# One branch behind the attention instead of three, the attention's bias on ScalarE, and the root's first operation moved

## The chip, the cores and the metric

The kernel runs on one core of a Trainium2 chip. The metric is the device time of one execution in microseconds (us). A core has five engines with queues of their own: TensorE (PE in the profile; its weight loads are PEld), VectorE (DVE), ScalarE (ACT), GpSimd (POOL) and SyncE (SP, which issues most transfers). An instruction runs when it is at the head of its engine's queue and the semaphores that it waits for have been raised by other engines or by transfers.

## The reference, cut to what matters

```python
def _attn_ref(q, k, v, n_global, n_local):          # batch 2, 8 heads, 768 positions, head_dim 64
    scores = scale * np.matmul(q, k.transpose(0, 1, 3, 2))
    is_global = pos[None, :] < int(n_global)        # 8
    is_local = (rel >= 0) & (rel < int(n_local))    # 96; rel = query position - key position
    dist = np.where(is_global & ~is_local, float(n_local), np.abs(rel))
    scores = scores - slopes[:, None, None] * dist
    scores = np.where(is_global | is_local, scores, -1000000000.0)
    a = softmax(scores)
    return np.matmul(a, v)

def _moe_ref(x, w_gate, w_val, w_out, rms_g):       # 1536 tokens, 512 -> 1536 -> 512
    xn = x / np.sqrt(np.mean(x * x, -1) + 1e-06) * rms_g
    g = xn @ w_gate
    return (silu(g) * (xn @ w_val)) @ w_out

def _moe2_ref(x, w_skip, w_gate, w1, w2):           # 8 experts, 512 -> 1024 -> 512, one per kept token
    ...
```

The two numbers n_global and n_local are inputs. The kernel has a windowed path for n_local up to 97 and n_global up to 32, and a general path for all other values. With the inputs that are timed (8 and 96) the general path is skipped.

## The kernel before, in words

The program is one long straight line in which the author fixes the order on each engine by the order of the Python calls. It has four stages, which the profile separates by time: the windowed attention (to about 99 us), the first products of the gated layer with the RMS statistics (to about 125 us), the rest of the gated layer and of the routing, and the experts.

**The start.** `load_ints` (L39) fetches the two integers, `consts` (L44 to L79) turns them into floats `gl` on DVE, and five small DVE operations (L70 to L76) make `fasti`, 1 when the windowed path applies. `values_load` (L77) reads it into a register of every engine, and `tc.If(flag == 0)` (L985) skips `general_attention`. `bias_tiles` (L94 to L117), a generator, then makes on DVE, from the table `rel` (576 columns of distances, 576 of key numbers, 8 slopes; L978 loads it), a mask `keep` and `miss`, a clipped distance, and for each of four pairs of heads four pieces of `bias` (L112), one `next` for a pair.

**The attention.** `attention` (L192 to L390) is a generator too. It works on 24 items (8 pairs of heads, 3 groups of 256 queries). In step t it issues the scores of item t on PE (`qk`, L240), transposes of item t-2 (`trans`, L286), the product with the values of item t-3 (`pv`, L313); on DVE the normalization of item t-1 (L267, L271, L278) and for item t four score operations (`ttr`, L251: score plus bias, and the row's extreme `m`); on ACT the exponentials (`exp`, L262). `tick()` between DVE operations takes one step of another generator, `s.small`: there the root of the RMS statistics is put among the score operations.

**The statistics.** `Rms.stats(g)` sums squares by PE products with ones (L444). Called with 3 it issues the first DVE operation of the root, `rv` (L448), at once. `Rms.root` (L450) is the generator of what follows: 11 small DVE operations on 128 x 6 and six diagonal tiles `rd`, three on DVE (L469) and three on ACT (L472). `spread` (L474) multiplies these with ones on PE (L478), and ACT copies the result to `rs` (L481).

**Behind the attention.** In the last steps PE begins the products of the gated layer (`gemm1`, L538); `gate1` (L549 to L556) closes each on DVE and ACT, one product behind (`behind`). A second `tc.If` stood after step 16 (L1048), a third after the attention (L1065); both use the register loaded at the start. Behind the third come the root of the second half, the fourth product, and `spread`.

Of the kernel before, what the change touches and what calls it, by code (L numbers as in the profile page):

```python
# [18 lines left out]
NEG = -1.0e9  # L19
# [24 lines left out]
def consts(s, ints):  # L44
# [23 lines left out]
    s.ng, s.nl = s.gl[:, 0:1], s.gl[:, 1:2]  # L68
    a = c.tile([128, 3], F32, name="fasta")
# [24 lines left out]
def bias_tiles(s):  # L94

    nc = s.nc
    s.kinds = [0, 64, 192, 384]
# [3 lines left out]
    keep, miss, slopes = s.keep, s.miss, s.slopes  # L103
    nc.gpsimd.tensor_copy(slopes, s.rel[:, 2 * N:])
    spans = [(0, 64, 0), (64, 192, 4), (192, 384, 0), (384, 576, 4)]
# [12 lines left out]
def general_attention(s):  # L118

    nc, tc = s.nc, s.tc  # L120
    with tc.tile_pool(name="ga", bufs=1) as p, tc.tile_pool(name="gap", bufs=1, space=PSUM) as ps:
        slopes = p.tile([128, 8, 2], F32, name="gslopes")
        for j in range(16):
            nc.gpsimd.memset(slopes[:, j // 2, j % 2:j % 2 + 1], -(2.0 ** -(j % 8 + 1)))
        with tc.For_i(0, 8, 1) as pr:
            slope = p.tile([128, 2], F32, name="gslope")
            nc.vector.tensor_copy(slope, slopes[:, ds(pr, 1), :].rearrange("p a b -> p (a b)"))
            for hh in range(2):
                r = slice(64 * hh, 64 * hh + 64)
                q = p.tile([64, 768], F32, name="gq")  # L130
                nc.sync.dma_start(q.rearrange("p (a n) -> p a n", a=1),
                                  s.qx.rearrange("a p n -> p a n")[r, ds(pr, 1), :])
                k = p.tile([64, 928], F32, name="gk")
                nc.sync.dma_start(k.rearrange("p (a n) -> p a n", a=1),
                                  s.kx.rearrange("a p n -> p a n")[r, ds(pr, 1), :])
                v = p.tile([128, 11, 64], F32, name="gv")
                nc.sync.dma_start(v.rearrange("p (a b) d -> p a b d", a=1),
                                  s.vx.rearrange("a p h b d -> p a h b d")[:, ds(pr, 1), hh])
                xo = p.tile([64, 768], F32, name="gxo")
                rel0 = p.tile([128, 768], F32, name="grel0")  # L140
                nc.gpsimd.iota(rel0, pattern=[[-1, 768]], base=0, channel_multiplier=1,
                               allow_small_or_imprecise_dtypes=True)
                key0 = p.tile([128, 768], F32, name="gkey0")
                nc.gpsimd.iota(key0, pattern=[[1, 768]], base=0, channel_multiplier=0,
                               allow_small_or_imprecise_dtypes=True)
                with tc.For_i(0, 6, 1) as i:
                    qi = p.tile([64, 128], F32, name="gqi")
                    nc.vector.tensor_scalar(qi.rearrange("p (a c) -> p a c", a=1),
                                            q.rearrange("p (i c) -> p i c", c=128)[:, ds(i, 1), :],
                                            0.125, None, ALU.mult)  # L150
                    rel = p.tile([128, 768], F32, name="grel")
                    nc.vector.tensor_copy(rel, rel0)
                    key = p.tile([128, 768], F32, name="gkey")
                    nc.vector.tensor_copy(key, key0)
                    loc = p.tile([128, 768], F32, name="gloc")
                    dist, keep = distance(s, rel, key, loc)
                    sc = ps.tile([128, 6, 128], F32, name="gsc")
                    for j in range(6):
                        nc.tensor.matmul(sc[:, j, :], lhsT=qi, rhs=k[:, 160 * j:160 * j + 128],
                                         start=True, stop=True)  # L160
                    t = p.tile([128, 768], F32, name="gt")
                    nc.vector.scalar_tensor_tensor(
                        out=t, in0=dist, scalar=slope[:, hh:hh + 1], in1=sc.rearrange("p a b -> p (a b)"),
                        op0=ALU.mult, op1=ALU.add)
                    nc.vector.tensor_tensor(t, t, keep, ALU.mult)
                    nc.vector.tensor_scalar(keep, keep, 1.0, -NEG, ALU.subtract, ALU.mult)
                    nc.vector.tensor_tensor(t, t, keep, ALU.add)
                    m = p.tile([128, 1], F32, name="gm")
                    nc.vector.tensor_reduce(m, t, AX.X, ALU.max)
                    nc.vector.tensor_scalar(t, t, m, None, ALU.subtract)  # L170
                    z = p.tile([128, 1], F32, name="gz")
                    nc.scalar.activation(t, t, AF.Exp, accum_out=z)
                    nc.vector.tensor_scalar(z, z, 1e-9, None, ALU.add)
                    nc.vector.reciprocal(z, z)
                    nc.vector.tensor_scalar(t, t, z, None, ALU.mult)
                    pt = ps.tile([128, 6, 128], F32, name="gpt")
                    for j in range(6):
                        nc.tensor.transpose(pt[:, j, :], t[:, 128 * j:128 * j + 128], s.ident)
                    pts = loc.rearrange("p (a b) -> p a b", a=6)
                    nc.vector.tensor_copy(pts, pt)  # L180
                    po = ps.tile([64, 128], F32, name="gpo")
                    for j in range(6):
                        nc.tensor.matmul(po, lhsT=v[:, 2 * j, :], rhs=pts[:, j, :],
                                         start=j == 0, stop=j == 5)
                    nc.vector.tensor_copy(xo.rearrange("p (i c) -> p i c", c=128)[:, ds(i, 1), :],
                                          po.rearrange("p (a c) -> p a c", a=1))
                    nc.vector.tensor_scalar(rel0, rel0, 128.0, None, ALU.add)
                nc.sync.dma_start(s.xg.rearrange("(a h p) n -> p a h n", h=2, p=64)[:, ds(pr, 1), hh, :],
                                  xo.rearrange("p (a n) -> p a n", a=1))
# [203 lines left out]
class Rms:  # L393
# [30 lines left out]
    def general(self, xg):  # L424

        s, nc = self.s, self.s.nc
        for hp in range(4):
# [3 lines left out]
            sq = self.sq[hp] if hp < 2 else s.rpool.tile([128, 768], F32, name="gsq", bufs=1)  # L431
# [3 lines left out]
            if hp > 1:  # L435
                nc.vector.tensor_tensor(self.sq[1], self.sq[1], sq, ALU.add)

    def stats(self, g, psum=None):
# [7 lines left out]
        if g == 3:  # L446
            self.v = s.rpool.tile([128, 6], F32, name="rv", bufs=2)
            nc.vector.tensor_scalar(self.v, self.ss[:, 0:6], 1.0 / 512.0, 1e-6, ALU.mult, ALU.add)  # L448

    def root(self):  # L450

        s, nc, v = self.s, self.s.nc, self.v
        r = s.r[self.b] = s.cpool.tile([128, 6], F32, name=f"r{self.b}")
# [12 lines left out]
        d = self.diag = s.rpool.tile([128, 6, 128], F32, name="rd", tag="sq", bufs=4)  # L466
# [475 lines left out]
def attn_moe_kernel(ctx, tc, qx, kx, vx, rel, ints, wgv, w_out, rms_g, w9, w9t, w1, w2, out):  # L942
# [33 lines left out]
    s.keep = s.apool.tile([128, 576], F16, name="keep", bufs=1)  # L976
# [4 lines left out]
    s.miss = s.apool.tile([128, 576], F32, name="miss", bufs=1)  # L981
# [44 lines left out]
    def step1(x, *parts, silu=True):  # L1026

        gemm1(s, *x)
        run(*parts, *[gate1(s, *behind.pop(0), silu) for _ in behind[:1]])
        behind.append(x)  # L1030

    def gemm1s():
        z = done[0]
        done[0] += 1
# [396 lines left out]
```

## Time and profile before

| | us |
|---|---|
| median of 3 runs (lowest, highest) | 554.08 (553.87, 554.45) |
| the profiled execution, its own time | 554.08 |
| its span, from first to last instruction | 552.3 |
| PE busy in the span | 524.2 (95%) |
| DVE busy | 404.8 (73%) |
| ACT busy | 277.5 (50%) |
| POOL busy | 140.8 (25%) |

The span is 1.8 us shorter than the execution's own time, and that execution's time is the median of the runs. Busy time is an average over the four stages; what a stage is bound by is read from its own stretch. In rows of the timeline the columns are the start in the span, the length, engine, line, operation, tiles, sizes and count, and in brackets the idle time of that engine just before with what ended it.

### The profile page before, as it was taken

To read this page: it belongs to the slowest core of one execution; us is meant where nothing else is said; L and a number is where in the kernel's file an instruction comes from. 1 tells how busy PE (TensorE), PEld (TensorE's weight loads), DVE (VectorE), ACT (ScalarE), POOL (GpSimd) and SP (SyncE) were. 2 spreads that over 40 slices of the span, in tenths; PEclk is the share of its full clock that TensorE was granted. 3 is DMA by queue.
4 is the path that set the end of the run, shared out by engine and by line. 5 is a ranking of instruction groups with operands and counts; after the bars stand their busy time and mean duration, and the time that the engine had idled before them with its cause. 6 is when DMAs were issued, how large, how long until landed. Compare 5 with 4: busy or idle time off the path is not lost. (4 is left out here: it accounts for less than half of the span.)

```text
span 552.3 us, 9096 instructions
## 1 busy us (share of the span) xinstructions
PE 524.2 (95%) x3132; PEld 425.8 (77%) x3132; DVE 404.8 (73%) x1026; ACT 277.5 (50%) x631; POOL 140.8 (25%) x140
## 2 busy tenths in 40 slices
PE   3899886999999999999999999999999999999994
PEld 2676665878888888888888888878789787888883
DVE  5899999567888688868884358456443599999971
ACT  2799896324332233333333255244231587988850
POOL 2446545001222212212220200000000512666001
PEclk9999998999999999999999999999999999999998
DMA  8653511112323323323313512116171599999300
GB/s 301 210 211 139 173 36 39 33 46 77 105 88 113 113 79 114 114 79 113 115 38 130 214 39 78 39 52 215 39 293 57 202 393 395 398 399 396 131 15 16
DMA packets 28997, 80.62 MB, mean 146 GB/s; under 512 B 3512, under 2 KB 3768, under 8 KB 28945
## 3 DMA queue, kind: packets, MB, share of 16 engines
q1 hardware_dynamic: 24400, 68.61, 35.0%
q0 software_dynamic: 2672, 8.22, 3.9%
q10 hardware_dynamic: 1872, 3.15, 1.6%
q8 instruction: 26, 0.43, 0.3%
q14 instruction: 27, 0.21, 0.1%
HBM read 72.28 MB, written 8.65 MB: 147 GB/s over the span
## 5 line engine op out<-in xcount | busy, mean ns | idle before, releaser
L538 PE MATMUL ps<-xh,wh 128*128 128x512 f32 (+1 forms) x304 | 115.4, 380 | 0.1
L538 PE MATMUL ps<-xh,wl 128*128 128x512 f32 (+1 forms) x304 | 115.0, 378 | 0.5 <-POOL wl L504 0.5
L538 PE MATMUL ps<-xl,wh 128*128 128x512 f32 (+1 forms) x304 | 114.9, 378 | 0.0
L854 DVE TENSOR_TENSOR ewl<-eraw,ewh 128x1024 fp32r<-128x1024 f32 x72 | 83.5, 1220 | 6.2 <-ACT ewh L845 5.9
L845 ACT CAST ewh<-eraw 128x1024 fp32r<-128x1024 f32 x72 | 71.3, 1055 | 6.2 <-DVE ewl L854 4.2
L538 PEld LDWEIGHTS ps<-xh,wl 128*128 128x128 f32 x304 | 57.2, 188 | 11.6 <-POOL wl L504 0.9
L491 DVE SCALAR_TENSOR_TENSOR wraw<-f64t,wraw 128x512 f32<-128x512 f32 x36 | 44.7, 1241 | 28.8 <-ACT f64t L489 28.8
L538 PEld LDWEIGHTS ps<-xh,wh 128*128 128x128 f32 x304 | 57.2, 188 | 11.0 <-issue 0.7
L538 PEld LDWEIGHTS ps<-xl,wh 128*128 128x128 f32 x304 | 57.2, 188 | 10.6
L604 PE MATMUL px<-woh,hh 128*128 128x512 f32 (+1 forms) x156 | 61.8, 396 | 0.0
L604 PE MATMUL px<-woh,hl 128*128 128x512 f32 (+1 forms) x156 | 58.7, 376 | 0.0
L604 PE MATMUL px<-wol,hh 128*128 128x512 f32 (+1 forms) x156 | 58.2, 373 | 0.0
L504 POOL TENSOR_TENSOR wl<-f64t,wh 128x512 fp32r<-128x512 f32 x24 | 31.0, 1293 | 101.3 <-ACT wh L503 55.7
L503 ACT CAST wh<-f64t 128x512 fp32r<-128x512 f32 x24 | 14.9, 622 | 71.4 <-DVE f64t L501 68.1
L262 ACT ACTIVATE es<-es,m 128x192 f32<-128x192 f32 (+1 forms) x96 | 41.4, 434 | 11.5 <-DVE m L251 10.3
L278 POOL TENSOR_SCALAR es<-es,z 128x192 f32<-128x192 f32 x46 | 36.0, 791 | 36.2 <-ACT pts L297 11.7
L286 PE MATMUL pt<-ident,es 128*128 128x128 f32 x176 | 30.5, 305 | 10.1 <-DVE pts L295 6.6
L286 PEld LDWEIGHTS pt<-ident,es 128*128 128x128 f32 x176 | 20.7, 152 | 21.6 <-DVE pts L295 10.0
L568 DVE TENSOR_TENSOR hl<-h,hh 128x256 fp32r<-128x256 f32 x72 | 25.4, 422 | 15.8 <-ACT hh L567 15.8
L604 PEld LDWEIGHTS px<-woh,hl 128*128 128x128 f32 x156 | 29.3, 188 | 5.8
L604 PEld LDWEIGHTS px<-woh,hh 128*128 128x128 f32 x156 | 29.4, 188 | 4.9
L604 PEld LDWEIGHTS px<-wol,hh 128*128 128x128 f32 x156 | 29.5, 189 | 4.0
(195 smaller groups left out, 979.7 us busy)
## 6 DMA issues: line engine op xcount, KB each, us to landing
eraw<-in_w_dram SPq DMA_DIRECT2D x64, 512.0 KB, 11.2
wraw<-in_wgv_dram SPq DMA_DIRECT2D x24, 512.0 KB, 3.8
wraw<-in_w_out_dram SPq DMA_DIRECT2D x12, 512.0 KB, 3.5
vp<-in_vx_dram SPq DMA_DIRECT2D x8, 704.0 KB, 4.0
eraw<-in_w_dram POOLq DMA_DIRECT2D x8, 512.0 KB, 13.6
kd<-in_kx_dram SPq DMA_DIRECT2D x7, 464.0 KB
xm<-x SPq DMA_DIRECT2D x12, 256.0 KB
out_dram<-x ACTq DMA_DIRECT2D x12, 256.0 KB, 2.8
```

Of the source, the lines that this page charges most:

```text
L262: nc.scalar.activation(e[:, r, x, e0:e0 + n], e[:, r, x, e0:e0 + n], AF.Exp, bias=m[:, j:j + 1], scale=-1.0, accum_out=z[:, j:j + 1])
L278: eng.tensor_scalar(e[:, r, x, e0:e0 + n], e[:, r, x, e0:e0 + n], z[:, j:j + 1], None, ALU.mult)
L286: nc.tensor.transpose(pt[:, kt, x, :], e[:, r, x, 128 * kt:128 * kt + 128], s.ident)
L491: nc.vector.scalar_tensor_tensor(out=a.bitcast(F32), in0=t, scalar=F64_LEAST, in1=a.bitcast(F32), op0=ALU.is_ge, op1=ALU.mult)
L503: nc.scalar.copy(hi, t)
L504: eng.tensor_tensor(lo, t, f(hi), ALU.subtract)
L538: nc.tensor.matmul(p, lhsT=w[:, k, :], rhs=x[c][:, k, a:b], start=n == 0, stop=n == 11)
L568: nc.vector.tensor_tensor(hl[:, i, :], src, f(hh[:, i, :]), ALU.subtract)
L604: nc.tensor.matmul(p, lhsT=h[:, k, :], rhs=w[k][:, c:c + N], start=n == 0, stop=n == 35)
L845: eng.copy(wh, raw)
L854: eng.tensor_tensor(wl, raw, f(wh), ALU.subtract)
```

## The change

It does five things. (1) The flag is no longer read at the start: `consts` ends at `gl`, the five flag operations become `windowed`, called behind step 3 of the attention, and the read and the one `tc.If` stand behind the attention. In it lies the whole general path, which recomputes everything that the windowed path had made. (2) The branch after step 16 is gone. (3) The bias: three DVE operations make one table `dist` (clipped distance plus a large number where masked), and each pair's bias is `dist` times a slope, on ACT in two pieces (256 and 320 columns), except the second piece of the first pair, which is on DVE. The table's columns are put in another order for that. (4) `rv` is no longer issued by `stats` but is the first step of `root`. (5) The gate of the third product, which had run behind the root of the second half, is run before the branch.

```diff
@@ consts @@
     s.ng, s.nl = s.gl[:, 0:1], s.gl[:, 1:2]
+def windowed(s):
+    nc, c = s.nc, s.cpool
     a = c.tile([128, 3], F32, name="fasta")
...
     nc.vector.tensor_copy(s.fasti, s.fast)
-    flag = nc.values_load(s.fasti[0:1, 0:1], min_val=0, max_val=1,
-                          skip_runtime_bounds_check_because="a comparison's result")
-    return flag
@@ bias_tiles @@
-    nc.vector.tensor_scalar(keep, rel, s.nl, None, ALU.is_lt)
-    nc.vector.scalar_tensor_tensor(out=keep, in0=key, scalar=s.ng, in1=keep, op0=ALU.is_lt, op1=ALU.max)
-    nc.vector.tensor_scalar(miss, keep, 1.0, -8.0 * NEG, ALU.subtract, ALU.mult)
-    nc.vector.tensor_scalar(rel, rel, s.nl, None, ALU.min)
+    nc.vector.tensor_scalar(dist, rel, s.nl, -256.0 * NEG, ALU.is_ge, ALU.mult)
+    nc.vector.scalar_tensor_tensor(out=dist, in0=key, scalar=s.ng, in1=dist, op0=ALU.is_ge, op1=ALU.mult)
+    nc.vector.scalar_tensor_tensor(out=dist, in0=rel, scalar=s.nl, in1=dist, op0=ALU.min, op1=ALU.add)
     for hp in range(4):
-        for a, b, z in spans:
-            nc.vector.scalar_tensor_tensor(out=s.bias[:, hp, a:b], in0=rel[:, a:b],
-                                           scalar=slopes[:, z + hp:z + hp + 1],
-                                           in1=miss[:, a:b], op0=ALU.mult, op1=ALU.add)
+        nc.scalar.activation(s.bias[:, hp, 0:256], dist[:, 0:256], AF.Copy, scale=slopes[:, hp:hp + 1])
+        if hp:
+            nc.scalar.activation(s.bias[:, hp, 256:N], dist[:, 256:N], AF.Copy, scale=slopes[:, 4 + hp:5 + hp])
+        else:
+            nc.vector.tensor_scalar(s.bias[:, hp, 256:N], dist[:, 256:N], slopes[:, 4:5], None, ALU.mult)
         yield
@@ Rms @@
-        if g == 3:
-            self.v = s.rpool.tile([128, 6], F32, name="rv", bufs=2)
-            nc.vector.tensor_scalar(self.v, self.ss[:, 0:6], 1.0 / 512.0, 1e-6, ALU.mult, ALU.add)
-    def root(self):
-        s, nc, v = self.s, self.s.nc, self.v
-        r = s.r[self.b] = s.cpool.tile([128, 6], F32, name=f"r{self.b}")
+    def root(self, diag=None):
+        s, nc = self.s, self.s.nc
+        v = s.rpool.tile([128, 6], F32, name="rv", bufs=2)
+        nc.vector.tensor_scalar(v, self.ss[:, 0:6], 1.0 / 512.0, 1e-6, ALU.mult, ALU.add)
+        yield
...
@@ attn_moe_kernel @@
     next(att)
-    flag = consts(s, ints)
+    consts(s, ints)
     bias = bias_tiles(s)
-    with tc.If(flag == 0):
-        general_attention(s)
...
     for t in att:
         if t < 3:
             next(bias)
+        if t == 3:
+            windowed(s)
...
-        if t == 16:
-            with tc.If(flag == 0):
-                rms[0].general(s.xg)
         if t == 17:
-            for g in range(4):
+            for g in range(3):
                 rms[0].stats(g)
             s.small = rms[0].root()
...
+    run(*[gate1(s, *behind.pop(0), silu=False) for _ in behind[:1]])
+    flag = nc.values_load(s.fasti[0:1, 0:1], min_val=0, max_val=1,
+                          skip_runtime_bounds_check_because="a comparison's result")
     with tc.If(flag == 0):
-        rms[1].general(s.xg)
+        general_attention(s)
+        rms[0].general(s.xg, s.h[1, 0].rearrange("p a b -> p (a b)")[:, 0:768])
...
         for g in range(3):
             rms[1].stats(g, ss)
-    rms[1].stats(3)
     run(rms[1].root())
```

In the order of each engine this stands at three places. A wait shown in brackets with a row names the engine (DVE_49, Activation_49, PE_49, Pool_49) whose semaphore has to be raised before that row may run.

The first place is ACT's queue at the start, up to the exponentials of the first item (`es`). Before:

```order
L985 UNCONDITIONAL_BRANCH [waits Activation_49]
L262 ACT_TABLE_LOAD
L262 ACTIVATE es_366,z<-es_366,m 128x64 [waits DVE_49]
L262 ACTIVATE es_366,z<-es_366,m 128x128 [waits DVE_49]
L262 ACTIVATE es_366,z<-es_366,m 128x192 [waits DVE_49] x2
```

And in the changed kernel:

```order
L982 DMA rg<-in_rms_g_dram 128x4
L111 ACT_TABLE_LOAD [waits DVE_49]
L111 ACTIVATE bias<-dist,slopes 128x256 [waits Pool_49]
L260 ACTIVATE es_159,z<-es_159,m 128x64 [waits DVE_49]
L260 ACTIVATE es_159,z<-es_159,m 128x128 [waits DVE_49]
L260 ACTIVATE es_159,z<-es_159,m 128x192 [waits DVE_49] x2
L111 ACTIVATE bias<-dist,slopes 128x256
L113 ACTIVATE bias<-dist,slopes 128x320
```

The load of the activation table had no wait of its own; now the first bias piece waits for two engines, and its wait for DVE (the third `dist` operation) stands ahead of the table load.

The second place is DVE's queue at the branch behind the attention: the gate of the second product (`h_365`, 256 columns), the branch, and the root of the second half. Before:

```order
L549 TENSOR_TENSOR h_365<-ps_1795,rs_338 128x256 [waits PE_49]
L554 TENSOR_TENSOR sg<-sg,h_365 128x256 [waits Activation_49]
L556 TENSOR_TENSOR h_365<-sg,ps_1808 128x256 [waits DVE_49,PE_49]
L1065 COMPARE_AND_BRANCH
...
L448 TENSOR_SCALAR rv<-ss 128x6 [waits PE_49]
...
L549 TENSOR_TENSOR h_364<-ps_1851,rs_332 128x512
L554 TENSOR_TENSOR sg<-sg,h_364 128x512 [waits Activation_49]
L556 TENSOR_TENSOR h_364<-sg,ps_1864 128x512 [waits DVE_49]
```

And in the changed kernel (`h_158` is the second product's gate, `h_157` the third's):

```order
L559 TENSOR_TENSOR h_158<-sg,ps_1554 128x256 [waits DVE_49,PE_49]
L552 TENSOR_TENSOR h_157<-ps_1597,rs_128 128x512 [waits PE_49]
L557 TENSOR_TENSOR sg<-sg,h_157 128x512 [waits Activation_49]
L559 TENSOR_TENSOR h_157<-sg,ps_1610 128x512 [waits DVE_49,PE_49]
L1068 TENSOR_LOAD fasti [waits DVE_49]
L1070 COMPARE_AND_BRANCH
...
L450 TENSOR_SCALAR rv<-ss 128x6 [waits PE_49]
```

The third product's gate has moved from behind the root to before the branch, and a read of the flag stands between it and the branch.

The third place is DVE's queue in the attention's step 18, where the first root begins. Before:

```order
L501 SCALAR_TENSOR_TENSOR f64t<-wraw,f64t 128x512
L448 TENSOR_SCALAR rv<-po 128x6
L267 TENSOR_SCALAR z<-z 128x4
L454 TENSOR_SCALAR r_1376<-rv 128x6
L271 RECIPROCAL z<-z 128x4
L456 TENSOR_SCALAR r_1376<-r_1376 128x6
L278 TENSOR_SCALAR es_368<-es_368,z 128x192
```

And in the changed kernel:

```order
L504 SCALAR_TENSOR_TENSOR f64t<-wraw,f64t 128x512
L265 TENSOR_SCALAR z<-z 128x4
L450 TENSOR_SCALAR rv<-po 128x6
L269 RECIPROCAL z<-z 128x4
L455 TENSOR_SCALAR r_1123<-rv 128x6
L276 TENSOR_SCALAR es_161<-es_161,z 128x192
L457 TENSOR_SCALAR r_1123<-r_1123 128x6
```

`rv` is now behind the first operation of the normalization, and every later operation of this root comes one DVE operation later.

## Rows read from the trace of the kernel before

**Rows 1.** Busy time by stretch, whole core (columns: length, engines, granted clock, DMA share).

```profile
0.00:125.00 125.00, 105.33 (x1094) 80.98 (x1095) 101.45 (x422) 84.30 (x290) 50.40 (x69) 0.97 0.38 131
125.00:305.00 180.00, 180.00 (x812) 149.79 (x812) 138.91 (x206) 60.63 (x112) 42.79 (x40) 1.00 0.31 101
```

**Rows 2.** Timeline of the first 23 us, DVE and ACT.

```profile
4.52 0.16 DVE L65 SCALAR_TENSOR_TENSOR gl<-intt,intw 128x2 f32<-128x2 f32 x1
5.21 0.15 DVE L76 CAST fasti<-fast 128x1 int32<-128x1 f32 x1
6.47 1.28 ACT L262 ACT_TABLE_LOAD   x1 [6.47 <-ACTq L985]
6.74 0.51 DVE L106 TENSOR_SCALAR keep<-rel,gl 128x576 f16<-128x576 f16 x1 [1.37 <-DVEq L985]
7.29 0.82 DVE L107 SCALAR_TENSOR_TENSOR keep<-rel,gl,keep 128x576 f16<-128x576 f16 x1
...
9.00 1.21 DVE L112 SCALAR_TENSOR_TENSOR bias<-rel,slopes,miss 128x64 f32<-128x64 f16 x4
10.12 0.22 DVE L251 CUSTOM_DVE_ANT_0 es<-sc,bias 128x64 f32<-128x64 f32 x1
...
11.12 0.44 ACT L262 ACTIVATE es<-es,m 128x192 f32<-128x192 f32 x1
...
22.92 0.36 DVE L251 CUSTOM_DVE_ANT_0 es<-sc,bias 128x192 f32<-128x192 f32 x1 [0.88 <-PE sc L240]
```

**Rows 3.** The read of the flag on DVE, and the first 4.5 us by stretch.

```profile
L77 DVEq TENSOR_LOAD <-fasti x1: 546/546/546, 5.4 to 5.4; - x1
...
0.00:4.50 4.50, 0.00 (x0) 0.00 (x0) 0.33 (x2) 0.00 (x0) 0.94 (x8) 1.00 0.41 101
```

**Rows 4.** Timeline near 318 us: a table load behind a wait for DVE.

```profile
318.22 0.15 DVE L674 TENSOR_SCALAR rm<-rm 128x1 f32<-128x1 f32 x1
318.45 1.28 ACT L677 ACT_TABLE_LOAD   x1 [2.59 <-DVE rm L674]
319.74 0.27 ACT L677 ACTIVATE rex<-lg,rm 128x8 f32<-128x8 f32 x1
```

**Rows 5.** Timeline of the attention's steps 18 and 19, around the first root.

```profile
68.09 1.27 POOL L504 TENSOR_TENSOR wl<-f64t,wh 128x512 fp32r<-128x512 f32 x1 [1.96 <-ACT wh L503]
68.37 0.17 DVE L448 TENSOR_SCALAR rv<-po 128x6 f32<-128x6 f32 x1 [1.01 <-PE po L444]
68.45 0.94 DVE L267 TENSOR_SCALAR z<-z 128x4 f32<-128x4 f32 x1
...
73.05 0.16 DVE L464 SCALAR_TENSOR_TENSOR r<-rt,r 128x6 f32<-128x6 f32 x1
...
73.24 0.99 ACT L472 ACTIVATE rd<-ident,r 128x128 f32<-128x128 f32 x3
```

**Rows 6.** Branch and flag reads on the queues themselves (duration in ns, start in us).

```profile
L1065 PEldq COMPARE_BRANCH  x1: 200/200/200, 114.6 to 114.6; - x1
...
L1339 DVEq TENSOR_LOAD <-eji x1: 322/322/322, 544.9 to 544.9; - x1
```

**Rows 7.** Timeline behind the attention, around the branch and the second root.

```profile
114.82 0.42 DVE L556 TENSOR_TENSOR h<-sg,ps 128x256 f32<-128x256 f32 x1
118.10 0.17 DVE L448 TENSOR_SCALAR rv<-ss 128x6 f32<-128x6 f32 x1 [2.86 <-PEq L1065]
...
121.18 0.68 DVE L549 TENSOR_TENSOR h<-ps,rs 128x512 f32<-128x512 f32 x1
...
123.29 0.69 DVE L556 TENSOR_TENSOR h<-sg,ps 128x512 f32<-128x512 f32 x1
...
122.84 0.71 PE L478 MATMUL rb<-rd,ones 128*128 128x128 f32 x4 [0.69 <-ACT rs L481]
```

**Rows 8.** The end of the attention: a pause of PE, and the stretch after it.

```profile
90.09 0.66 PE L286 MATMUL pt<-ident,es 128*128 128x128 f32 x4 [1.68 <-DVE pts L295]
...
92.00:99.00 7.00, 4.67 (x36) 3.91 (x32) 5.79 (x12) 2.11 (x6) 1.86 (x2) 0.51 0.01 2
```

More of the change, by code (lines that the diff above doesn't have):

```diff
@@ L118, in general_attention @@
 def general_attention(s):
[L120 to L141, printed above, removed]
@@ new lines, in general_attention @@
+    nc, tc, p = s.nc, s.tc, s.apool
+    slopes = p.tile([128, 8, 2], F32, name="gslopes", bufs=1)
+    for j in range(16):
+        nc.gpsimd.memset(slopes[:, j // 2, j % 2:j % 2 + 1], -(2.0 ** -(j % 8 + 1)))
+    one, two = (s.h[c, 0].rearrange("p a b -> p (a b)") for c in range(2))
+    rel, key = one[:, 0:768], two[:, 0:768]
+    qi, xo = one[0:64, 768:896], one[0:64, 896:1024]
+    ks = [two[0:64, 768 + 128 * j:896 + 128 * j] for j in range(2)]
+    ks += [s.rs[2][0:64, 128 * j:128 * j + 128] for j in range(4)]
@@ L142, in general_attention @@
                                allow_small_or_imprecise_dtypes=True)
-                key0 = p.tile([128, 768], F32, name="gkey0")
-                nc.gpsimd.iota(key0, pattern=[[1, 768]], base=0, channel_multiplier=0,
+                nc.vector.tensor_scalar(rel, rel, first, None, ALU.add)
+                nc.gpsimd.iota(key, pattern=[[1, 768]], base=0, channel_multiplier=0,
                                allow_small_or_imprecise_dtypes=True)
[L146 to L161, printed above, removed]
-                    nc.vector.scalar_tensor_tensor(
[L163 to L187, printed above, removed]
@@ L188, in general_attention @@
-                nc.sync.dma_start(s.xg.rearrange("(a h p) n -> p a h n", h=2, p=64)[:, ds(pr, 1), hh, :],
-                                  xo.rearrange("p (a n) -> p a n", a=1))
+                dist, keep = distance(s, rel, key, loc)
+                for h in range(2):
+                    sc = s.ps_g.tile([128, 3, 128], F32, name="gsc", tag="ps0", bufs=2)
+                    for j in range(3):
+                        nc.tensor.matmul(sc[:, j, :], lhsT=qi, rhs=ks[3 * h + j], start=True, stop=True)
+                    c = slice(384 * h, 384 * h + 384)
+                    nc.vector.scalar_tensor_tensor(
+                        out=t[:, c], in0=dist[:, c], scalar=slope[:, hh:hh + 1],
+                        in1=sc.rearrange("p a b -> p (a b)"), op0=ALU.mult, op1=ALU.add)
@@ L192, in attention @@
+                for j in range(6):
+                    nc.tensor.matmul(po, lhsT=v[:, 2 * j, :], rhs=pts[:, j, :], start=j == 0, stop=j == 5)
+                nc.vector.tensor_copy(xo, po)
+                nc.sync.dma_start(
+                    s.xg.rearrange("(a h p) (i c) -> p a h i c", h=2, p=64, c=128)[:, ds(pr, 1), hh, ds(i, 1), :],
+                    xo.rearrange("p (a b c) -> p a b c", a=1, b=1))
+                nc.vector.tensor_scalar(first, first, 128.0, None, ALU.add)
 def attention(s, rms):
@@ L430, in general @@
             nc.sync.dma_start(x, xg[r:r + 128, :])
[L431 removed]
+            sq = s.rpool.tile([128, 768], F32, name="gsq", bufs=1) if hp else sums
             for g in range(3):
@@ L1030, in step1, with first @@
         behind.append(x)
+    def first(z):
+        return (z // 2, 1, 0, 256) if z % 2 else (z // 2, 0, 0, 512)
     def gemm1s():
@@ L1064, in attn_moe_kernel @@
             rms[1].stats(2)
+    run(*[gate1(s, *behind.pop(0), silu=False) for _ in behind[:1]])
+    flag = nc.values_load(s.fasti[0:1, 0:1], min_val=0, max_val=1,
+                          skip_runtime_bounds_check_because="a comparison's result")
     with tc.If(flag == 0):
-        rms[1].general(s.xg)
+        general_attention(s)
+        rms[0].general(s.xg, s.h[1, 0].rearrange("p a b -> p (a b)")[:, 0:768])
+        ss0 = s.bank([128, 133], "ss")
+        for g in range(3):
+            rms[0].stats(g, ss0)
+        run(rms[0].root(s.rpool.tile([128, 6, 128], F32, name="gx", bufs=1)))
+        for z in range(3):
+            rms[0].spread(z, s.bank([128, 256], "rb"))
+        for z in range(done[0]):
+            gemm1(s, *first(z))
+            run(gate1(s, *first(z), silu=False))
+        rms[1].general(s.xg, rms[1].sq[0])
         for g in range(3):
             rms[1].stats(g, ss)
-    rms[1].stats(3)
     run(rms[1].root())
```

63 lines of the change are left out of this document (51 added, 12 removed).

## The prediction

> **What bounds the kernel now.** I read the busy time by stretch first. In the 180 us behind 125 us PE is busy for 180.00 us [rows 1]: nothing that DVE, ACT or POOL gain there counts, and a time won or lost before 125 us is carried to the end unchanged. All five parts of the change lie before 125 us, where PE is busy for only 105 of 125 us and DVE for 101 [rows 1]. So the sum is about waits in three places, and the second view is the timeline there. At the start it shows DVE idle for 1.37 us until the branch at L985 releases it, then four operations for the bias, the first pair's bias, and the first score operation at 10.12 us [rows 2]; the attention is a chain from there, so that start is what the first part can move. In step 18 it shows DVE waiting 1.01 us for the sums of squares on PE [rows 5]. Behind the attention it shows DVE waiting 2.86 us for the branch on PE's queue, and PE waiting 0.69 us for an ACT copy [rows 7]. The third view is the rows of the queues themselves, which tell when flag reads and branches run [rows 3, 6].
>
> **The start: a gain of 1.3 us.** In the change DVE goes on from `gl`, which ends at 4.52 + 0.16 = 4.68 us [rows 2]. The table `rel` is needed too: it is the first large transfer, 290 KB, and by 4.5 us the queues had moved 4.5 x 101 = 455 KB [rows 3], so I take it as there; if not, the next operation would wait, up to 0.5 us by my estimate. Three operations on 576 columns replace four. The first is like L106 (0.51 us), the two with three operands like L107 (0.82) [rows 2]. With 0.04 us between operations they end at 4.72 + 0.51 + 0.04 + 0.82 + 0.03 + 0.82 = 6.94 us. Now the order matters: in ACT's queue the table load stands behind the wait for the third of them. Elsewhere in this trace just that form appears: the DVE operation ends at 318.37, the load starts at 318.45, takes 1.28, and the activation starts at 319.74 [rows 4]. The load that ran beside other work at 6.47 us [rows 2] is thus put on the path: 6.94 + 0.08 + 1.28 + 0.01 = 8.31 us. The first bias piece has 256 columns. An exponential of 192 took 0.44 [rows 2]; scaled, 256 take between 0.44 and 0.59, and I take 0.50. The first score operation follows at 8.31 + 0.50 + 0.03 = 8.84 us, in place of 10.12: a gain of 1.28 us. DVE's own piece (320 columns) is done meanwhile. Bounds: with `rel` late 0.8, with a first operation and a piece at their shortest 1.5. Removing the flag read and the branch alone would have given 6.74 - 4.72 = 2.02, and dropping the fourth operation and the four pieces more; the table load eats the difference.
>
> [...]
>
> **The other bias pieces, and the flag operations: nothing.** For pairs 1 to 3 DVE loses 1.21 us a step [rows 2] and ACT gains about 0.5 + 0.6 us. DVE's pieces ran while it waited for the exponentials anyway, and ACT's run while it waits for DVE's next score operation. Without that cover they cost up to three times 1.1 = 3.3 us; I see no cause for that, since DVE needs its own four steps before ACT can go on. The five flag operations took from 4.68 to 5.36 us, 0.68 [rows 2]. Behind step 3 they lie in front of a DVE wait of 0.88 us for PE [rows 2], so 0; bound 0.7.
>
> **Step 18 and the branch after step 16: nothing.** What DVE gains by losing the branch falls into its 1.01 us of waiting for PE's sums [rows 5]: 0. Then the first operation of the normalization, `z`, no longer stands behind `rv`. Behind it, it ran from 68.45 to 69.39 instead of 0.17 us, until POOL's subtraction ended at 69.36 [rows 5]; ahead of it, it runs before 68.09. But `rv` still waits for PE until 68.37, and the root's next operations, of the same kind as `z`, then meet POOL. I take a gain of 0.2 us. Against it, every operation of the root comes one score operation later: the last before the diagonal tiles ended at 73.21, and ACT's three tiles followed at 73.24 [rows 5]. Now ACT gets them some 0.4 us later. ACT is busy without a break there, so up to 0.4 can be lost; I set the two against each other, 0, with bounds of -0.3 and +0.4.
>
> **The branch behind the attention: a gain of 0.3 us.** The third product's gate took from 121.18 to 123.98, 2.80 us, behind the root [rows 7]. In the change it begins at 114.82 + 0.42 = 115.24, fills the 2.86 us in which DVE waited [rows 7], and ends at 118.04. New is the flag read. PE's queue does not wait for PE's work: its branch ran at 114.6, while its sums of squares let `rv` go only at 118.10 [rows 6, 7]. So PE reads the flag ahead. DVE's queue runs one operation ahead: it can read the flag when the gate's last operation (0.69 us) has started, at 117.35. A read took between 0.32 and 0.55 us [rows 3, 6]; then come the branch and the jump, which at the start took from 5.4 + 0.55 to 6.74, some 0.8 us [rows 2, 3]. That gives 118.5 to 118.7 for `rv`, against 118.10: a loss of about 0.4. PE's fourth product waits for DVE's and ACT's passage as well and moves with it. In return ACT no longer runs that gate's sigmoid ahead of its copies, and PE's wait of 0.69 us [rows 7] goes, because the copy is done while PE still works on the second pair of tiles: 0.4 - 0.69 = -0.3. Bounds: a passage at no cost gives -0.7; one that only begins when the gate has ended costs what the start showed, 5.36 to 6.74, 1.38 us [rows 2], hence +0.7.
>
> **Sum.** -1.28 + 0 + 0 - 0.3 = -1.6 us. The profiled execution took 554.08 us, which is also the median, so the forecast is **552.5 us**. Bounds added up: 554.08 - 1.5 - 0.3 - 0.7 = 551.6 and 554.08 - 0.8 + 0.4 + 0.7 = 554.4; that all bad ones come together is unlikely, so the forecast's own range is 551.7 to 553.5.
>
> **The rivals.**
> *The table load is not held back.* If ACT loads the table before the wait, it is done long before 6.94 us, and the sum is 1.28 us better: 551.2. For it: at 6.47 it ran unbidden [rows 2]. Against: the order puts the wait ahead of it, and [rows 4] shows what that does.
> *The flag costs in full behind the attention.* DVE and PE read, branch and jump one after the other, +1.38 - 0.69 = +0.7 in place of -0.3: 553.5, within 0.2% of before (about 1.1 us, what a measurement of this kernel can tell from no change). For it: the start. Against: PE's branch at 114.6 [rows 6].
> [...]
> [...]
> [...]
>
> **How the numbers follow.** Forecast 0.62, table load not held back 0.07, flag in full 0.13, whole price 0.05, clock 0.08; 0.05 is left for what I do not name, on either side. Faster by over 0.2% means below 552.97: three quarters of the forecast's case (0.47), the first rival (0.07), a third of the second (0.04) and a part of the rest, 0.60. Slower: the clock and a little, 0.09. Within 0.2%: 0.31. The range runs from the first rival, 551.1, to the edge of the third, 553.9.
>
> **What would show it.** In the profile after: `dist` starting near 4.7 us and ending near 6.9; the table load starting right behind it and taking 1.28; the first score operation near 8.8. PE's flag read some 2 to 3 us before its sums of squares end; `rv` of the second root about 0.4 us later than the end of the sums; no wait of PE for an ACT copy before the third `rb` product. If the first score operation stands near 7.6, the table load was not held; if near 10, it costs more than its row. If all of this holds and the time is still 554, the gain was lost inside the attention: then steps 4 to 24 are longer, with PE or ACT late where DVE was.

## The result: 5.0 us slower, nearly all of it at the branch

| | before | after |
|---|---|---|
| median of 4 runs each (us) | 553.98 | 559.0 |
| lowest to highest (us) | 551.13 to 554.45 | 558.52 to 559.8 |
| the profiled execution: own time, span (us) | 554.08, 552.3 | 559.33, 557.6 |

The ratio is 1.0103, with a 95% interval of 1.0067 to 1.0139: slower by 1%. The kernel before has an execution between 551.1 and 552.0 us now and then (here the one of 551.13); all others, here and below, lie between 553.8 and 555.7. The forecast was 552.5, its range 551.1 to 553.9. The busy time by stretch of the changed kernel shows where to look; it answers to [rows 1], with two short stretches more:

```profile
0.00:125.00 125.00, 102.78 (x1062) 77.97 (x1063) 97.97 (x406) 85.02 (x293) 49.98 (x69) 0.95 0.37 131
125.00:305.00 180.00, 179.98 (x822) 150.43 (x821) 135.95 (x199) 60.28 (x108) 41.32 (x32) 0.99 0.28 94
118.00:121.00 3.00, 0.00 (x0) 0.00 (x0) 0.00 (x0) 0.00 (x0) 0.00 (x0) 0.89 0.03 8
121.00:126.30 5.30, 5.22 (x24) 5.25 (x25) 3.02 (x16) 0.99 (x3) 0.00 (x0) 0.50 0.01 2
```

From 118 to 121 us no engine computes anything, and in the 5.3 us behind that PE has its lower clock level (a granted clock of 0.50).

The timeline behind the attention, PE and DVE (it answers to [rows 7]):

```profile
116.81 1.06 PE L443 MATMUL ss<-ones,sq 128*128 128x128 f32 x8
117.25 0.69 DVE L559 TENSOR_TENSOR h<-sg,ps 128x512 f32<-128x512 f32 x1
121.03 0.17 DVE L450 TENSOR_SCALAR rv<-ss 128x6 f32<-128x6 f32 x1 [3.09 <-DVEq L1070]
121.08 0.55 PE L541 MATMUL ps<-xh,wh 128*128 128x256 f32 x1 [3.22 <-DVEq L1070]
...
126.34 2.18 PE L481 MATMUL rb<-rd,ones 128*128 128x128 f32 x12
...
128.27 0.37 PE L541 MATMUL ps<-xh,wh 128*128 128x256 f32 x1
```

The same three places in the kernel before, PE (fourth product, first `rb`, next product):

```profile
118.12 0.36 PE L538 MATMUL ps<-xh,wh 128*128 128x256 f32 x1
...
121.07 1.08 PE L478 MATMUL rb<-rd,ones 128*128 128x128 f32 x8
...
123.31 0.36 PE L538 MATMUL ps<-xh,wh 128*128 128x256 f32 x1
```

So the loss divides into three: the product begins 121.08 - 118.12 = 2.96 us later; it takes 126.34 - 121.08 = 5.26 in place of 121.07 - 118.12 = 2.95 us, 2.31 more, at the lower clock; and from `rb` to the next product it is 1.93 in place of 2.24 us, 0.31 less, because PE's wait of 0.69 us for ACT's copy is gone, though the first `rb` products still ran at the lower clock (0.50 from 126.34 to 126.90 us). Together 4.96 us, which PE carries to the end: its last product ends at 549.77 instead of 544.85. The spans differ by 5.3 us; the rest lies behind that last product.

The rows of the queues show what the 3 us are (duration in ns, start in us; they answer to [rows 6]):

```profile
L1068 DVEq TENSOR_LOAD <-fasti x1: 544/544/544, 117.3 to 117.3; - x1
...
L1070 PEldq COMPARE_BRANCH  x1: 3542/3542/3542, 115.1 to 115.1; - x1
L1070 ACTq EVENT_SEMAPHORE  x1: 17/17/17, 116.8 to 116.8; - x1
L1070 DVEq COMPARE_BRANCH  x1: 72/72/72, 117.9 to 117.9; - x1
...
L1070 DVEq EVENT_SEMAPHORE  x1: 21/21/21, 120.9 to 120.9; - x1
```

DVE read the flag while its last operation ran, took the branch at 117.9, and did its next thing, a semaphore, at 120.9. PE's branch alone took 3.54 us, from 115.1 on, mostly beside its own work; ACT's jump, begun at 116.3, was over at 116.8. PE's fourth product waits for DVE's passage.

The start, DVE, ACT and POOL (it answers to [rows 2]):

```profile
4.96 1.33 DVE L107 TENSOR_SCALAR dist<-rel,gl 128x576 f32<-128x576 f16 x1 [0.35 <-DMA rel<-in_rel_dram]
5.05 0.93 POOL L332 MEMSET es<- 128x128 f32 x6
...
8.08 1.28 ACT L111 ACT_TABLE_LOAD   x1 [8.08 <-DVE dist L109]
9.38 0.51 ACT L111 ACTIVATE bias<-dist,slopes 128x256 f32<-128x256 f32 x1
9.92 0.22 DVE L249 CUSTOM_DVE_ANT_0 es<-sc,bias 128x64 f32<-128x64 f32 x1 [1.42 <-ACT bias L111]
```

The first score operation stands at 9.92 in place of 10.12 us: 0.20 gained, not 1.28.

### The profile page after: what moved, and what is told of

Read it like the earlier page. It is cut to its first block, busy times and chain, and to the rows that moved or that the text cites. A ratio compares the mean times of both kernels' runs of the same rounds, so it can differ in the third digit from the quotient of the medians.

```text
span 557.6 us, 9071 instructions
## 1 busy us (share of the span) xinstructions
PE 526.3 (94%) x3132; PEld 427.6 (77%) x3132; DVE 401.3 (72%) x1010; ACT 280.2 (50%) x638; POOL 140.2 (25%) x140
## 5 line engine op out<-in xcount | busy, mean ns | idle before, releaser
L541 PE MATMUL ps<-xh,wh 128*128 128x512 f32 (+1 forms) x304 | 116.9, 385 | 3.2 <-DVEq L1070 3.2
L541 PE MATMUL ps<-xh,wl 128*128 128x512 f32 (+1 forms) x304 | 116.4, 383 | 0.4 <-POOLq L1070 0.4
L541 PE MATMUL ps<-xl,wh 128*128 128x512 f32 (+1 forms) x304 | 116.3, 383 | 0.0
L541 PEld LDWEIGHTS ps<-xh,wh 128*128 128x128 f32 x304 | 58.5, 192 | 14.5 <-issue 3.9
L541 PEld LDWEIGHTS ps<-xh,wl 128*128 128x128 f32 x304 | 58.4, 192 | 11.6 <-POOLq L1070 0.9
L541 PEld LDWEIGHTS ps<-xl,wh 128*128 128x128 f32 x304 | 58.5, 192 | 10.4
L559 DVE TENSOR_TENSOR h<-sg,ps 128x512 f32<-128x512 f32 (+1 forms) x38 | 24.8, 652 | 15.2 <-PE ps L541 8.1
```

Source lines behind the costliest of these rows:

```text
L541: nc.tensor.matmul(p, lhsT=w[:, k, :], rhs=x[c][:, k, a:b], start=n == 0, stop=n == 11)
L559: nc.vector.tensor_tensor(u, sg, ps[1], ALU.mult)
```

## The experiments

Theory J: the time is the jump over the long body. That the code behind it has to be fetched first was the author's guess at a reason. Its rival F: it is the read of the flag, and the join behind it. Theory C: the pause is what lets PE's clock fall.

**No branch.**

```diff
-    flag = nc.values_load(s.fasti[0:1, 0:1], ...)
-    with tc.If(flag == 0):
-        ...
```

> The changed kernel without the read of the flag and without the branch behind the attention: the general path is left out. Theory J (the jump over the long body costs the time) and theory F (the read of the flag and the join cost it) both take the pause of 3.2 us of PE away. Theory C says that the pause is also what lets PE's clock fall behind it (2.3 us in the fourth product): then the window 121 to 126 shows the full clock and the time is 559.0 - 3.1 - 2.3 = 553.6 us. If the clock falls there for another reason, 555.9 us.

Measured: 554.51 us (552.65 to 555.3), ratio to before 0.9991 (0.9974 to 1.0008). The fourth product follows the sums of squares without a pause, at the full clock (1.00 from 115 to 126 us). So pause and low clock go together with the branch. The time is 0.9 above the expectation: in the profiled execution PE lost 1.08 us at 246.4 in a wait for DVE, which had waited for ACT, and ACT for a transfer of weights. That stall is not in the next run's profile, and it stays unexplained.

**A short body at the same place.**

```diff
     with tc.If(flag == 0):
-        general_attention(s)
-        rms[0].general(...)
-        ...
         rms[1].general(s.xg, rms[1].sq[0])
```

> The flag is read and the branch taken at the same place, but the body holds only the second half's squares and sums (17 instructions of DVE in place of 125, 8 of PE in place of 149); the general attention, the first half's part and the three products of the general path are left out. J: DVE's queue passes in 0.4 to 0.7 us as the third branch of the kernel before did, the second root's first operation starts near 118.6, PE's pause is about 0.7 us and the clock stays full: 554.2 us. F: nothing changes, PE's pause stays near 3 us: 558.5 to 559.0 us.

Measured: 553.32 us (553.02 to 553.77), ratio to before 0.9974 (0.9964 to 0.9985), 0.9 below the expectation. Queue rows of this run:

```profile
L1068 DVEq TENSOR_LOAD <-fasti x1: 543/543/543, 117.2 to 117.2; - x1
...
L1070 PEldq COMPARE_BRANCH  x1: 228/228/228, 115.0 to 115.0; - x1
...
L1070 DVEq COMPARE_BRANCH  x1: 72/72/72, 117.9 to 117.9; - x1
L1070 DVEq EVENT_SEMAPHORE  x1: 21/21/21, 118.1 to 118.1; - x1
```

The read, the branch and the join are those of the changed kernel, and DVE is through in 0.2 us in place of 3.0. F falls as an explanation of the 3 us. The DMA view of 112 to 122 us has transfers of instructions (queue and kind, packets, MB, share of 16 engines), first of the changed kernel, then of the kernel before; with the short body it has none:

```profile
q8 instruction: 2, 0.03, 1.2%
q14 instruction: 4, 0.03, 1.1%
```

```profile
q14 instruction: 4, 0.03, 0.9%
```

Of the six in the changed kernel two lie about 1 us behind PE's branch (116.0 and 116.1) and one about 1 us behind DVE's (119.0). That the engines wait for these is the author's guess; the rows give 3.0 us for DVE's passage and 3.5 for PE's, and no reason. A transfer is not yet a wait. One lies 1.1 us behind ACT's branch too (117.4), and ACT had gone on at 116.8; the kernel before has four, and there DVE took 0.5 us from its branch to its next semaphore (114.9 to 115.4). So the body's length is shown to cost the 3 us, and that they are spent on a fetch is not shown.

**The flag read early.**

```diff
+        if t == 5:
+            flag = nc.values_load(s.fasti[0:1, 0:1], ...)
     ...
-    flag = nc.values_load(s.fasti[0:1, 0:1], ...)
     with tc.If(flag == 0):
```

> The whole body, but each engine reads the flag behind step 5 of the attention, so that only the comparison stands at the branch. J: DVE's read ran beside the gate's last operation, so the jump starts at the same time or 0.05 us earlier and takes 3.0 us again: 558.5 to 559.0 us. F: the read's 0.54 us and what hangs on it go: PE's pause falls to 2.5 us or less, 556.0 to 558.4 us.

Measured: 556.01 us (555.25 to 557.96), ratio to before 1.0035 (1.0012 to 1.0057). The number lies at the lower edge of F's range, and the rows say why it is not F:

```profile
L1071 DVEq COMPARE_BRANCH  x1: 72/72/72, 117.4 to 117.4; - x1
...
L1071 DVEq EVENT_SEMAPHORE  x1: 21/21/21, 120.5 to 120.5; - x1
```

The jump takes 3.1 us as before. But it begins 0.5 us earlier, so J was wrong that the read hides beside the gate. PE's pause is 2.69 us instead of 3.22, and now the clock stays full in the fourth product (1.00 from 121 to 126 us). Half a microsecond of pause and 2.3 us of clock make most of the 3.0 us.

```profile
121.00:126.00 5.00, 4.99 (x43) 4.79 (x42) 2.68 (x15) 2.26 (x7) 0.00 (x0) 1.00 0.01 2
```

That is the profiled execution, 556.12 us. Of the eight, five lie at 555.3 to 556.1 with a mean granted clock of 0.989 or 0.990, and three at 557.6 to 558.0 with 0.983 or 0.984, the level of the changed kernel (0.977 to 0.984). By that the clock fell in some executions of this kernel and not in others.

**The third product's gate behind the branch.**

```diff
...
-    run(*[gate1(s, *behind.pop(0), silu=False) for _ in behind[:1]])
     flag = nc.values_load(...)
     with tc.If(flag == 0):
         ...
-        for z in range(done[0]):
+        for z in range(2):
         ...
```

The rest of the edit gives the general path other PSUM banks and keeps the third product's result for the gate behind the branch.

> The whole branch stays, but the third product's gate goes back behind it, as in the kernel before (the general path then leaves the third product out and uses other PSUM banks). DVE comes to the branch at about 115.2 instead of 117.9. J: DVE's 3.0 us run beside PE's sums of squares and end near 118.7, PE's own passage (3.5 us from 115.1) ends near 118.7; the pause is about 1 us, the clock stays full, and the 0.69 us wait for the ACT copy is back: 559.0 - 2.2 - 2.3 + 0.5 = 555.0 us. If the passage begins only when PE has done its sums (117.9), the pause stays near 3 us: 559 us or more.

Measured: 555.6 us (555.23 to 556.42), ratio to before 1.0025 (1.0007 to 1.0042). DVE's jump ran from 115.9 to 118.9 and PE's 3.46 us from 115.6, both beside PE's last products and sums of squares (to 118.35); PE's pause is 0.99 us and the clock stays full (1.00 from 118 to 126 us). Here the passage was covered, since both queues got to the branch while PE still had work.

**Idle products over the pause.** This is for C: the pause is filled and the jump left alone.

```diff
+    idle = s.bank([128, 512], "idle")
+    for z in range(10):
+        nc.tensor.matmul(idle, lhsT=s.w[0, 0][0][:, 0, :], rhs=s.xh[0][:, 0, :], start=True, stop=True)
     flag = nc.values_load(...)
```

> The changed kernel with ten idle products of 512 columns on PE between the sums of squares and the branch (their result is not used). By the trace of the changed kernel they keep PE busy from 117.9 to about 120.2, while DVE and the branch are as before. Theory C (the pause makes the clock fall): PE's pause shrinks to about 1 us, the clock stays full in the fourth product, and its 24 matmuls take 2.9 us instead of 5.2: 559.0 - 2.3 = 556.7 us, up to 557.4 if PE's own passage of the branch is now the later one. If the clock falls for another reason than the pause: 559 us.

Measured: 557.03 us (553.67 to 557.69), within the expectation. DVE's jump took 3.0 us again, PE's pause was 0.94 us, and the fourth product ran at the full clock (1.00 from 118 to 126 us).

```profile
120.59 0.35 PE L541 MATMUL ps<-xh,wh 128*128 128x256 f32 x1 [0.94 <-DVEq L1073]
```

The profiled execution is one of the faster ones, 555.7 us; of the others only the mean granted clock is known, 0.987 or more in all but one (0.983). C holds in this run: the same passage with PE at work cost no clock.

**Two branches in place of one.**

```diff
     with tc.If(flag == 0):
         general_attention(s)
+    with tc.If(flag == 0):
         rms[0].general(...)
```

> The whole general path stays, but in two branches on the same flag, one behind the other: the attention in the first, all the rest in the second, so that each engine takes two jumps of about half the length (DVE about 58 and 67 instructions). J with a limit on the length: both jumps take 0.2 to 0.5 us, PE's pause is below 1 us, the clock stays full: 553.3 to 554.5 us. If the code behind the first jump must be fetched all the same, one of the two takes 3 us on DVE: 558.5 to 559.5 us.

Measured: 558.64 us (558.15 to 559.74), no better than the change. The queues' rows:

```profile
L1070 DVEq COMPARE_BRANCH  x1: 72/72/72, 118.3 to 118.3; - x1
L1070 DVEq EVENT_SEMAPHORE  x1: 21/21/21, 118.9 to 118.9; - x1
...
L1072 DVEq COMPARE_BRANCH  x1: 56/56/56, 119.0 to 119.0; - x1
...
L1072 DVEq EVENT_SEMAPHORE  x1: 21/21/21, 121.5 to 121.5; - x1
```

The first jump took 0.6 us, the second, right behind it, 2.5. Two jumps of half the length, one behind the other, cost DVE what the one long jump did. Why the first was short and the second long no run shows.

**POOL's fills ahead.** In this run and the next the start is taken apart; the branch is left as it is.

```diff
+    es += [...]; nc.gpsimd.memset(es[z]...)
     yield
-    es += [...]; nc.gpsimd.memset(es[z]...)
```

> The changed kernel with POOL's six fills of the tile es ahead of the constants, so that they are over before the table rel lands. Theory M (POOL's fills hold back DVE's first operation for dist, which took 1.33 us instead of 0.51): the operation takes 0.5 to 0.55 us, dist ends near 7.2 instead of 8.0, the first score operation is near 9.1 instead of 9.92. Rival: the operation is slow by its form (16-bit in, 32-bit out): it takes 1.3 us again and nothing moves. The time: 558 to 559.5 us in both.

Measured in a single run: 557.99 us.

```profile
0.79 0.91 POOL L331 MEMSET es<- 128x128 f32 x6 [0.29 <-POOLq L1433]
...
5.03 0.52 DVE L107 TENSOR_SCALAR dist<-rel,gl 128x576 f32<-128x576 f16 x1 [0.47 <-DMA rel<-in_rel_dram]
...
9.17 0.22 DVE L249 CUSTOM_DVE_ANT_0 es<-sc,bias 128x64 f32<-128x64 f32 x1 [1.43 <-PE sc L238]
```

The operation takes 0.52 us once POOL is quiet. In the changed kernel it took 1.33 us and ended at 6.29, 0.31 us after POOL's last fill (5.05 + 0.93 = 5.98): 0.81 us were lost beside the fills. How the fills hold it back no run shows.

**The table load ahead as well.**

```diff
+    warm = s.cpool.tile([128, 1], F32, name="warm")
+    nc.vector.memset(warm, 0.0)
+    nc.scalar.activation(warm, warm, AF.Exp)
```

> As the run with the fills ahead, and ACT also runs one exponential on one number at the very start, so that its table is loaded before the wait for dist. If the table load held the start back by 1.28 us, the first score operation comes 1.3 us earlier than in that run, near 7.8 us where POOL's fills mattered and 8.6 where not. How much of it reaches the end of the attention: all of it (2.1 us) if the attention is a chain from its start; less if PE's clock or the transfers set the first steps. With the branch as it is the time is then 557 to 559 us.

Measured: 555.36 us (551.09 to 556.84), ratio to before 1.0017 (0.9992 to 1.0042).

```profile
1.24 1.28 ACT L985 ACT_TABLE_LOAD   x1 [1.24 <-PEq L1436]
...
7.31 0.51 ACT L111 ACTIVATE bias<-dist,slopes 128x256 f32<-128x256 f32 x1 [4.57 <-DVE dist L109]
...
7.85 0.23 DVE L249 CUSTOM_DVE_ANT_0 es<-sc,bias 128x64 f32<-128x64 f32 x1
```

The score operations begin 1.32 us earlier than with the fills alone, 2.07 earlier than in the change. The last step's `z` is 1.64 us earlier than in the change (88.03 against 89.67), and the sums of squares end 2.56 us earlier (115.31 against 117.87). The time is lower than expected: in the profiled execution (553.81 us, the second fastest of ten) PE paused 3.07 us at the branch and the clock did not fall (1.00 from 118 to 126 us). What it did in the others is not known.

**The branch hint.** One instruction more on PE and on DVE.

```diff
+    tc.mark_branch_hint_location("rare", hint="LikelyTaken", engines=[mybir.EngineType.PE, mybir.EngineType.DVE])
     ...
     flag = nc.values_load(...)
-    with tc.If(flag == 0):
+    with tc.If(flag == 0, label="rare"):
```

> The changed kernel, in which PE and DVE get one more instruction ahead: a branch hint that names the branch behind the attention as likely taken (it lands at the start of each queue's program). J says that the 3 us are the fetch of the code behind the body after the jump. If the hint makes the engine fetch it ahead, both jumps take 0.2 to 0.6 us, PE's pause is below 1 us and the clock stays full: 553.3 to 554.5 us. If a hint so far ahead is not kept, nothing changes: 558.5 to 559.5 us.

Measured: 554.0 us (553.74 to 555.05), ratio to before 0.9997 (0.9983 to 1.0011): the 5 us are gone, with the whole body in its place.

```profile
L1071 PEldq COMPARE_BRANCH  x1: 402/402/402, 115.5 to 115.5; - x1
...
L1071 DVEq COMPARE_BRANCH  x1: 84/84/84, 118.3 to 118.3; - x1
...
L1071 DVEq EVENT_SEMAPHORE  x1: 21/21/21, 118.9 to 118.9; - x1
```

PE's branch takes 0.40 instead of 3.54 us, DVE's jump 0.6 instead of 3.0, PE's pause is 0.78 us. SP got no hint, and from its branch to its first semaphore it takes 3.4 us here and 3.5 in the changed kernel (86.7 to 90.2):

```profile
L1071 SPq EVENT_SEMAPHORE  x8: 17/17/17, 90.4 to 90.9; - x8
L1071 SPq COMPARE_BRANCH  x1: 50/50/50, 87.0 to 87.0; - x1
```

The hint runs at 0.8 us, 117 us ahead of DVE's branch, and acts all the same. This settles where the time is: in the passage of this one jump, for with the body in its place and the hint alone added it is gone. It does not settle how. The DMA view of 112 to 122 us still has four of the six transfers of instructions:

```profile
q14 instruction: 3, 0.02, 0.7%
q8 instruction: 1, 0.02, 0.6%
```

One lies between 116 and 117 us, behind PE's branch (115.5), and one between 119 and 121, behind DVE's (118.3), and the passages are short all the same. Over the whole span there are 53, and 54 in the changed kernel. That the hint had the code fetched ahead is seen in no transfer: J's jump is shown, J's fetch stays a guess.

**Versions that beat both.** The start's two edits with the gate behind the branch, and with the hint (the diffs are those above, put together).

> Two edits of earlier runs together, with the whole general path but for the third product's gate: POOL's fills and ACT's table load ahead of the wait for dist, and the third product's gate behind the branch. Each alone gave 3.6 us (555.4) and 3.4 us (555.6) against 559.0. J with the measured rows: the start gives 1.3 us to the end of the attention beside the two edits' 2 us at most, the passage costs 1 us of PE's pause at the full clock: 553.5 us, and so about 1 us below the kernel before (554.5). If the gain of the start is lost to PE's low clock at the end of the attention: 555.0 us, no gain against before.

Measured: 552.64 us (550.8 to 553.85), ratio to before 0.9964 (0.9951 to 0.9978), 0.9 below the expectation.

> The whole general path, the branch hint on PE and DVE, and POOL's fills and ACT's table load ahead of the wait for dist. From the rows: the sums of squares end 3 us earlier than with the hint alone (115.3 in place of 118.3, as in the run with start and gate), the passage costs 0.8 us at the full clock, and PE does not wait for an ACT copy: 554.0 - 3.0 + 0.3 = 551.3 us, 3 us below the kernel before. If the start's gain is lost to the low clock at the end of the attention this time: 553.0 us.

Measured: 552.09 us (549.19 to 552.72), ratio to before 0.9954 (0.9938 to 0.9971): 2.4 us below the kernel before and 6.9 below the change, with the whole general path in place. The sums of squares ended at 115.83 rather than 115.3, so 0.5 us of the start was lost on the way.

```profile
114.77 1.06 PE L443 MATMUL ss<-ones,sq 128*128 128x128 f32 x8
```

**The root's first operation put back.**

```diff
             s.small = rms[0].root()
+            next(s.small)
```

> The changed kernel with the root's first operation put back ahead of step 18's normalization. The prediction's 0 says that step 18's first operation z comes about 1 to 2 us later, behind rv and POOL's subtraction, and that steps 20 to 24 start at the same time as with the root among the score operations, within 0.4 us, when counted from step 17; the time stays at 559 us. Rival: the root's move is worth its 2.3 us of step 18 to the end: steps 20 to 24 come 1 us or more later.

Measured in a single run: 557.12 us. Step 18 of the attention in this run, then in the changed kernel (they answer to [rows 5]):

```profile
63.47 0.16 DVE L265 TENSOR_SCALAR z<-z 128x4 f32<-128x4 f32 x1
...
68.12 0.16 DVE L450 TENSOR_SCALAR rv<-po 128x6 f32<-128x6 f32 x1 [1.26 <-PE po L443]
68.20 0.68 DVE L265 TENSOR_SCALAR z<-z 128x4 f32<-128x4 f32 x1
...
76.13 0.17 DVE L265 TENSOR_SCALAR z<-z 128x4 f32<-128x4 f32 x1
```

```profile
62.85 0.17 DVE L265 TENSOR_SCALAR z<-z 128x4 f32<-128x4 f32 x1
...
66.16 0.17 DVE L265 TENSOR_SCALAR z<-z 128x4 f32<-128x4 f32 x1
...
75.69 0.17 DVE L265 TENSOR_SCALAR z<-z 128x4 f32<-128x4 f32 x1 [0.19 <-ACT es L260]
```

From step 17 to step 20 it is 76.13 - 63.47 = 12.66 us with the operation put back, and 75.69 - 62.85 = 12.84 as changed (12.80 to 12.84 in the other runs). Step 18 comes earlier (66.16 against 68.20), and all of it is given back, with 0.2 us on top: the root's move is worth nothing. That this run is 1.9 us below the change is not the root's doing: the fourth product ends 1.83 us earlier (124.51 against 126.34). Of this 0.55 us are an earlier end of the sums of squares, though this run's attention ended later (90.11 against 89.67), and 1.2 are the clock. PE's pause was 3.13 us here, and the lower level held for a shorter stretch (0.66 on average from 121 to 126): the product's matmuls came every 0.12 us until 121.96, then every 0.21.

## Why the prediction was wrong, step by step

- **The branch behind the attention, forecast -0.3, measured +4.96 us.** The step that failed is the sentence "then come the branch and the jump, which at the start took from 5.4 + 0.55 to 6.74, some 0.8 us". The price was taken from another branch over another body, and the upper bound of +0.7 from that same one. Here DVE jumps over 125 instructions and PE over 149, and that took 3.0 and 3.5 us; over 17 and 8 it took 0.2 each. The size of the body, which is the change itself, did not enter the sum. The pause of 3.2 us that came of it brought 2.31 us more by the clock. That PE and DVE read the flag ahead, that the third product's gate fits before the branch (it ended at 117.94, forecast 118.04), and that the 0.69 us wait goes were right; that the read itself costs some 0.5 us on DVE was in the sum too, and the run with the flag read early shows it. One line was read two ways: `[2.86 <-PEq L1065]` is not a wait for the branch, which PE had passed at 114.8, but for the semaphore behind PE's sums, as the branch's own paragraph has it.
- **"Clock", chance 0.08, is what happened.** Behind a pause of 3.22 us the fourth product ran at a granted clock of 0.50, and that cost 2.31 us. The passage that makes the pause was taken as 1.38 us at most in place of 3.1. At what pause the clock falls stays open: pauses of 2.69 and 3.07 us left the clock full (1.00), pauses of 3.10, 3.22 and 3.41 brought the lower level (0.50) at once, one of 3.13 for a part of the product. With two runs so close on both sides, and the kernel with the flag read early on either, whether the length alone decides no run shows. The range ended at 553.9, so the slower times, chance 0.09, lay outside it.
- **The start, forecast -1.28, measured -0.20 us.** Two assumptions failed. "I take it as there": `rel` landed after `gl`, and the first operation began at 4.96, not 4.72, 0.24 lost (the bound allowed for that). "The first is like L106 (0.51 us)": it took 1.33, behind POOL's fills, 0.82 lost. Before, the same fills began in the same moment as L106 (6.74 us), and it was they that took longer, 1.09 us in place of 0.91 alone; now POOL was ahead, since it had converted the slopes from 4.92 on. 8.84 + 0.24 + 0.82 = 9.90, and the trace says 9.92; so the rest of that sum was right. That POOL's fills are the cause the run with the fills ahead shows (0.52 us, all else alike). The table load was held behind the wait and took 1.28 us, and the bias began 0.02 us behind it (8.08 + 1.28 = 9.36, the bias at 9.38), which decides the first rival. The chance of 0.05 for a "whole price", and the range's edge of 553.9 with it, stand on a price above the load's own, which no run shows; the runs showed 1.28 us and nothing behind it. The prediction's own sign would have misled here: it took a first score operation near 10 us to mean that the table load costs more than its row.
- **Step 18 and the branch after step 16, forecast 0.** Right: the changed kernel is ahead by 0.87 us at step 16 (59.38 against 60.25) and by 0.96 at the end of the attention (89.67 against 90.63); in between it is up to 2.29 ahead, at step 18.
- **"A time won or lost before 125 us is carried to the end unchanged".** From the branch on this holds: 4.96 us at the next product, 4.92 at PE's last. Inside the first 125 us it does not: of the 0.96 us at the attention's end 0.11 is left at the sums of squares (116.81 against 116.92). PE had its lower clock in both kernels near 92 to 99 us (0.57 on average in the changed kernel, [rows 8] before). Before, the first product began just behind that stretch, at 99.14 (1.00 on average from there to 100.5, first matmul 0.50 us); in the changed kernel it began inside it, at 98.41 (0.50 to 99.84, first matmul 0.79 us). Other kernels with the same start reached the last step's `z` between 89.94 and 90.69, so part of the 0.96 belongs to this execution alone.

## What to carry to other kernels

A branch over a rarely used path cost DVE 0.2 to 0.6 us here where the body was short, and 3.0 us over the long one; PE took 3.5 us over it, while ACT and POOL passed the same branch in 0.5 and 0.8. Before several small branches are made into one, read in the queue rows, engine by engine, how long it is from the branch to the next instruction. The number of instruction transfers around a branch does not tell it: six with the long jump, but four in the kernel before and four with the hint. At which length a jump becomes a long one no run shows. Such a jump was made cheap by a hint (0.6 us on DVE, 0.40 on PE), or covered by work that PE still had (a pause of 0.99 us in place of 3.22). And where an operation is moved, its new neighbours on other engines belong to its price: here POOL's fills took 0.8 us of a start whose gain was forecast at 1.3.

## What the runs showed that was not expected

- A branch hint in the first microsecond shortened a jump 117 us later, PE's from 3.54 to 0.40 us.
- Two jumps in a row cost as much as one long one: 0.6 and 2.5 us on DVE.
- Pauses of nearly one length ended differently: 3.07 us left the clock full in one run, 3.10 us brought the lower level before the product began, and behind 3.13 us the product ran at the full clock for 1.5 us before it fell.
